# Converting 64-bit weights in blocks of 512 columns instead of 256, with two temporaries in the dead halves of the words

## The chip, the cores and the metric

The kernel runs on one core of a Trainium2 chip. The metric is the device time of one execution in microseconds (us), median over runs.

## What is computed

Attention with a feature map, then an ELU network whose weights come as float64, then a mixture of four experts (no biases):

```python
# attention: 4 batches, 8 heads, 576 tokens, 64 dims, 128 features
proj = einsum('bhsd,df->bhsf', x, w_phi);  proj -= max(abs(proj), -1)
phi = concatenate([exp(proj), exp(-proj)], -1)          # of q and of k
num = q_p @ (k_p^T v);  den = q_p @ sum(k_p) + 1e-6;  x = num / den
# ELU network: 2304 tokens, 512 -> 2048 -> 512, w_in and w_out float64
h = x @ w_in
g = where(h > 0, h, exp(minimum(h, 0)) - 1)
x = (g @ w_out).astype(float32)
# experts: E = 4, 512 -> 1024 -> 512, p = domain_probs normed
out += p[:, e:e+1] * (maximum(x @ w1[e], 0) @ w2[e])
```

## The kernel before

Activations and weights that TensorE multiplies are mostly split into a high part (fp32r) and the rest, so a product is three matmuls.

**Attention** works on 16 pairs of heads (`pair`, L171). A pair projects k and q (L194 in fp32 for the first seven pairs, L196 to L198 after), DVE takes the absolute maximum and subtracts it (`guard`, L204, L205, into `md`, `kp`, `qd`), ACT takes exponentials, TensorE forms k^T v (L237, L238), transposes q (L244) and forms numerator and denominator (L316), DVE divides (L325 reciprocal, L328 product into `xf`), and `put_x` splits `xf` into the tiles `xh` (ACT, L302) and `xl` (POOL, L303). A batch is four pairs.

**The ELU network** has 9 tiles of 256 tokens and runs in two halves of 4 units (`Elu`); a unit has 24 matmuls up (L525 to L527) and 24 down (L554 to L556). Between them ACT and DVE form `g` (L533, L534, L536) and its two parts `gh` (L537, ACT) and `gl` (L538, on POOL for the first three tiles, then on DVE). The down product of a unit is issued after the up product of the next. The first ELU unit needs the four pairs of batch 0.

**The experts** (`Up`, `Down`) fill the time from about 660 us on.

**Weights of the ELU network** are float64 in HBM, 32 tiles of 128 x 512 (16 of `w_in`, 16 of `w_out`). The chip has no float64 arithmetic here: `convert64` (L100) loads the words as 64-bit integers and builds the two fp32 parts from the upper and lower 32 bits, `hi` and `lo`, each of which is every other 32-bit word of the tile. Per block: one DMA (L102), ACT L108, L114 and L119, DVE L110 to L113, POOL L116, L118 and L121. `weight_stream` (L410) keeps up to `CVB` = 3 blocks in progress and advances one of them by a step at each call of `next(weights)`. Half of the 32 tiles fit in the ring of 16 (`RING`), so 32 blocks of 256 columns are converted at the start, beside attention, and the rest when the first half's weights are released, beside the last tiles of the first half and the start of the second. The calls come from two places: `PRE` calls at every step of attention until batch 0 is done (L747), then `WRATE` calls at every slot (L724).

The program is written as one stream; a scheduler of the tile framework then sets each engine's order of instructions, which all engines keep. Pools of buffers (`cv`, three of each tag) add waits: a load into `w64` waits for the last reader of the tile three blocks ago.

Of the kernel before, what the change touches and what calls it, by code (L numbers as in the profile page):

```python
# [8 lines left out]
F32 = mybir.dt.float32  # L9
F32R = mybir.dt.float32r  # L10
U32 = mybir.dt.uint32
I64 = mybir.dt.int64
ACTF = mybir.ActivationFunctionType
ALU = mybir.AluOpType
# [5 lines left out]
P = 128  # L20
# [24 lines left out]
LAG = 1  # L45
RING = 16
ATT_LAG = 5
PRE = 2
RATE = 1.4
WRATE = 2  # L50
CVB = 3
TAIL = 3
NF32 = 7
LDB = 1
CVP = 16
CVW = 256
CVOFF = 0
MINF = 2.0 ** -15
MAXF = 122879.9921875
# [3 lines left out]
def attn_elu_moe_kernel(ctx: ExitStack, tc: tile.TileContext, kq_in, vv, w_phi, w_in, w_out, probs, w1, w2, out):  # L63
    nc = tc.nc
    V, A, G, PE, SP = nc.vector, nc.scalar, nc.gpsimd, nc.tensor, nc.sync
    on = {'V': V, 'G': G}

    def f32(ap):
        return ap.bitcast(F32)

    def pool(name, bufs=1, stack=ctx, **kw):
        return stack.enter_context(tc.tile_pool(name=name, bufs=bufs, reuse_waits="tile", **kw))
# [14 lines left out]
    cv = pool("cv", CVB, stack=right, side="right")  # L87
# [12 lines left out]
    def convert64(dst, src, adder):  # L100
        st = cv.tile([P, CVW], I64, tag="w64", name="w64")
        SP.dma_start(st, src)  # L102
        words = st.bitcast(U32).rearrange("p (n two) -> p n two", two=2)
        lo, hi = words[:, :, 0], words[:, :, 1]
        top = cv.tile([P, CVW], U32, tag="top", name="top")
        pw = cv.tile([P, CVW], U32, tag="pw", name="pw")
        low = cv.tile([P, CVW], F32, tag="low", name="low")
        A.activation(f32(top), f32(hi), ACTF.Abs)  # L108
        yield
        V.tensor_scalar(out=f32(top), in0=f32(top), scalar1=MINF, scalar2=MAXF, op0=ALU.max, op1=ALU.min)  # L110
        V.tensor_scalar(out=top, in0=top, scalar1=3, scalar2=0x3FFFFFF8, op0=ALU.logical_shift_left, op1=ALU.bitwise_and)
        V.scalar_tensor_tensor(out=top, in0=hi, scalar=0xC0000000, in1=top, op0=ALU.bitwise_and, op1=ALU.bitwise_or)
        V.tensor_scalar(out=pw, in0=top, scalar1=0xFF800000, scalar2=None, op0=ALU.bitwise_and)  # L113
        A.activation(low, lo, ACTF.Copy, scale=2.0 ** -52)  # L114
        yield
        G.tensor_tensor(out=low, in0=low, in1=f32(pw), op=ALU.mult)  # L116
        yield
        adder.tensor_tensor(out=f32(top), in0=f32(top), in1=low, op=ALU.add)  # L118
        A.activation(dst[:, 0], f32(top), ACTF.Copy)  # L119
        yield  # L120
        G.tensor_tensor(out=dst[:, 1], in0=f32(top), in1=f32(dst[:, 0]), op=ALU.subtract)  # L121
# [241 lines left out]
    def ring_tile(key):  # L363
        rings[key] = ring.tile([P, 2, 512], F32R, tag="w", name="w")
        users.append(key)
# [34 lines left out]
    def conversions():  # L400
        for u in range(FP):
            for nm, src in (("in", w_in), ("out", w_out)):
                for f in (2 * u, 2 * u + 1):
                    while not room():
                        yield None
                    ring_tile((nm, f))
                    for o in range(0, 512, CVW):
                        yield convert64(rings[nm, f][:, :, o:o + CVW], src[f][:, o:o + CVW], G if f < CVP else V), (nm, f, o)

# [308 lines left out]
    def slot():  # L718
        quota[0] += rate[0]
        while quota[0] >= 1:  # L720
            quota[0] -= 1
            if done[0] < limit[0]:
                next(stream, None)
        for _ in range(WRATE):  # L724
            next(weights, None)
# [19 lines left out]
    while done[0] < NP:  # L745
        next(stream)
        for _ in range(PRE):  # L747
            next(weights)
# [134 lines left out]
```

## Time and profile before

| | us |
|---|---|
| median of three runs (1425.01 to 1426.37) | 1425.17 |
| the profiled execution | 1424.05 |
| its span, first to last instruction | 1422.3 |
| TensorE busy | 1380.5 |
| DVE busy | 698.2 |
| ACT busy | 619.9 |
| POOL busy | 446.7 |

The granted clock of TensorE is 0.997 of full speed over the span. PE is TensorE's matmuls and PEld its weight loads; DVE is VectorE, ACT ScalarE, POOL GpSimd, SP the engine that issues the DMAs. Matmuls are pipelined, so their spans overlap: a busy PE can still run below its pace. Spans on POOL are rough. A group's "idle before" says what the engine had been waiting for.

### The profile page before, as it was taken

What the parts mean: (1) busy time and instruction counts of PE and PEld (TensorE: products, weight loads), DVE (VectorE), ACT (ScalarE), POOL (GpSimd) and SP (SyncE); (2) the same over time, 40 slices, a digit from 0 to 9 for tenths busy, and PEclk for the clock granted to TensorE, in tenths of its full rate; (3) what the DMA queues carried; (4) which work ended last, traced back from release to release, by engine and by line L of the source; (5) the groups of instructions that cost most, each with busy time, mean ns of one, the idle gap of its engine ahead of it and who ended that gap; (6) DMA issues with size and microseconds to landing.
All of it is one profiled execution on the core that took longest, in us unless ns stands there. A gap on an engine that the chain in (4) does not pass through costs nothing.

```text
span 1422.3 us, 22325 instructions
## 1 busy us (share of the span) xinstructions
PE 1380.5 (97%) x8688; PEld 1286.9 (90%) x8688; DVE 698.2 (49%) x1150; ACT 619.9 (44%) x1348; POOL 446.7 (31%) x499
## 2 busy tenths in 40 slices
PE   7889999999999999999999999999999999999998
PEld 6788999999988999998898989898888989899897
DVE  7998856575588534333434323234432325323332
ACT  6777776665656544343333443122421214322121
POOL 5567654434588512033102350002320004300000
PEclk9999999999999999999999999999999999999999
DMA  5433222120423345313333233434145251433421
GB/s 162 128 118 117 88 66 77 40 74 24 128 90 118 112 143 191 108 46 104 114 131 148 94 106 135 160 112 148 45 149 181 105 196 52 141 111 133 167 78 67
DMA packets 93625, 160.22 MB, mean 113 GB/s; under 512 B 28496, under 2 KB 39888, under 8 KB 93520
## 3 DMA queue, kind: packets, MB, share of 16 engines
q1 hardware_dynamic: 93520, 158.80, 33.7%
q8 instruction: 68, 1.11, 0.3%
q14 instruction: 37, 0.30, 0.1%
HBM read 109.22 MB, written 49.55 MB: 112 GB/s over the span
## 4 chain that ended last, share of the span: by engine, by line
PE 74%; DVE 11%; DMA 5%; POOL 4%; issue 3%; ACT 3%; SPq 0%; DVEq 0%; POOLq 0%; ACTq 0%
PE bank L701 8%; PE bank L702 8%; PE bank L703 8%; PE bank L642 8%; PE bank L643 7%; PE bank L644 7%; PE bank L555 3%; PE bank L556 3%; PE bank L554 3%; PE bank L527 3%; PE bank L525 3%; PE bank L526 3%; PE bank L237 2%; PE bank L316 2%; DMA wst<-in_w 2%
## 5 line engine op out<-in xcount | busy, mean ns | idle before, releaser
L701 PE MATMUL bank<-w,h 128*128 128x512 f32 x576 | 224.5, 392 | 4.0 <-ACT h L653 4.0
L642 PE MATMUL bank<-xv,w 128*128 128x384 f32 x672 | 224.3, 340 | 3.1 <-ACT cm L648 2.9
L643 PE MATMUL bank<-xv,w 128*128 128x384 f32 x672 | 226.6, 337 | 0.0
L702 PE MATMUL bank<-w,h 128*128 128x512 f32 x576 | 225.5, 392 | 0.0
L644 PE MATMUL bank<-xv,w 128*128 128x384 f32 x672 | 223.4, 338 | 0.0
L703 PE MATMUL bank<-w,h 128*128 128x512 f32 x576 | 198.3, 391 | 0.7 <-DVE h L654 0.7
L462 POOL TENSOR_TENSOR w<-wst,w 128x256 fp32r<-128x256 f32 x80 | 62.2, 796 | 341.0 <-ACT w L461 336.9
L555 PE MATMUL bank<-gl,w 128*128 128x256 f32 x576 | 162.3, 286 | 6.3 <-DVE gl L538 5.0
L556 PE MATMUL bank<-gh,w 128*128 128x256 f32 x576 | 160.9, 284 | 0.0
L554 PE MATMUL bank<-gh,w 128*128 128x256 f32 x576 | 156.3, 288 | 3.9 <-ACT gh L537 3.4
L642 PEld LDWEIGHTS bank<-xv,w 128*128 128x128 f32 x672 | 126.6, 188 | 11.1 <-ACT cm L648 3.5
L654 DVE SCALAR_TENSOR_TENSOR h<-bank,h 128x384 fp32r<-128x384 f32 x144 | 77.4, 554 | 115.1 <-ACT h L653 115.1
L653 ACT ACTIVATE h<-bank 128x384 fp32r<-128x384 f32 x144 | 66.8, 490 | 151.6 <-PE bank L644 91.7
L701 PEld LDWEIGHTS bank<-w,h 128*128 128x128 f32 x576 | 108.5, 188 | 25.1 <-ACT h L653 5.3
L643 PEld LDWEIGHTS bank<-xv,w 128*128 128x128 f32 x672 | 126.8, 189 | 4.4
L702 PEld LDWEIGHTS bank<-w,h 128*128 128x128 f32 x576 | 108.6, 189 | 20.6
L644 PEld LDWEIGHTS bank<-xv,w 128*128 128x128 f32 x672 | 126.3, 188 | 0.0
L703 PEld LDWEIGHTS bank<-w,h 128*128 128x128 f32 x576 | 107.3, 188 | 20.0 <-DVE h L654 1.6
L555 PEld LDWEIGHTS bank<-gl,w 128*128 128x128 f32 x576 | 110.1, 191 | 9.6 <-DVE gl L538 7.5
L554 PEld LDWEIGHTS bank<-gh,w 128*128 128x128 f32 x576 | 106.1, 191 | 6.8 <-ACT gh L537 6.5
L556 PEld LDWEIGHTS bank<-gh,w 128*128 128x128 f32 x576 | 110.1, 191 | 0.2
L648 ACT ACTIVATE cmab<-bank 128x384 f32<-128x384 f32 x48 | 23.6, 492 | 178.0 <-PE bank L644 178.0
(119 smaller groups left out, 2991.0 us busy)
## 6 DMA issues: line engine op xcount, KB each, us to landing
xv<-xvd SPq DMA_DIRECT2D x42, 768.0 KB, 4.4
wst<-in_w SPq DMA_DIRECT2D x64, 256.0 KB, 2.8
xvd<-xv SPq DMA_DIRECT2D x21, 768.0 KB, 4.4
yscr<-y SPq DMA_DIRECT2D x54, 256.0 KB, 2.3
y<-yscr SPq DMA_DIRECT2D x54, 256.0 KB, 2.9
w<-in_w_in SPq DMA_DIRECT2D x32, 256.0 KB, 2.8
w<-in_w_out SPq DMA_DIRECT2D x32, 256.0 KB, 3.0
kq<-in_kq SPq DMA_DIRECT2D x16, 320.0 KB, 3.0
```

What stands on the lines that cost most here:

```text
L462: on[WL[v % len(WL)]].tensor_tensor(out=lo, in0=x, in1=f32(hi), op=ALU.subtract)
L554: PE.matmul(o, w[:, 0, c], self.gh[:, j], start=start, stop=False)
L555: PE.matmul(o, w[:, 0, c], self.gl[:, j], start=False, stop=False)
L556: PE.matmul(o, w[:, 1, c], self.gh[:, j], start=False, stop=stop)
L642: PE.matmul(o, hi[:, c], x[:, 0, kc], start=not more and kc == 0, stop=False, skip_group_check=more)
L643: PE.matmul(o, hi[:, c], x[:, 1, kc], start=False, stop=False, skip_group_check=more)
L644: PE.matmul(o, lo[:, c], x[:, 0, kc], start=False, stop=kc == 1, skip_group_check=more)
L653: A.activation(h[:, 0], c, ACTF.Relu)
L654: V.scalar_tensor_tensor(out=h[:, 1], in0=c, scalar=0.0, in1=f32(h[:, 0]), op0=ALU.max, op1=ALU.subtract)
L701: PE.matmul(self.acc, h[:, 0, c], w[:, 0], start=f == 0, stop=False)
L702: PE.matmul(self.acc, h[:, 0, c], w[:, 1], start=False, stop=False)
L703: PE.matmul(self.acc, h[:, 1, c], w[:, 0], start=False, stop=f == 2 * NQ - 1)
```

## The change

A block has 512 columns (`CVW`), a whole weight tile, so there are 32 blocks instead of 64 and each of the ten instructions handles twice the columns. The temporaries `pw` and `low` are gone: L113 writes the power of two into `hi`, which nobody reads after L112, and L114 writes the scaled low word over `lo`, in place; L116 and L118 read and write there. So the loaded tile is in use until L118, where it was free after L112 and L114. `PRE` and `WRATE` go from 2 to 1, which keeps the columns per call. `WRATE` also paces the later preparation of `w1` and `w2`. In the changed file all lines from 106 on have numbers lower by two.

```diff
-PRE = 2
+PRE = 1
-WRATE = 2
+WRATE = 1
-CVW = 256
+CVW = 512
...
         top = cv.tile([P, CVW], U32, tag="top", name="top")
-        pw = cv.tile([P, CVW], U32, tag="pw", name="pw")
-        low = cv.tile([P, CVW], F32, tag="low", name="low")
         A.activation(f32(top), f32(hi), ACTF.Abs)
         yield
...
         V.scalar_tensor_tensor(out=top, in0=hi, scalar=0xC0000000, in1=top, op0=ALU.bitwise_and, op1=ALU.bitwise_or)
-        V.tensor_scalar(out=pw, in0=top, scalar1=0xFF800000, scalar2=None, op0=ALU.bitwise_and)
-        A.activation(low, lo, ACTF.Copy, scale=2.0 ** -52)
+        V.tensor_scalar(out=hi, in0=top, scalar1=0xFF800000, scalar2=None, op0=ALU.bitwise_and)
+        A.activation(f32(lo), lo, ACTF.Copy, scale=2.0 ** -52)
         yield
-        G.tensor_tensor(out=low, in0=low, in1=f32(pw), op=ALU.mult)
+        G.tensor_tensor(out=f32(lo), in0=f32(lo), in1=f32(hi), op=ALU.mult)
         yield
-        adder.tensor_tensor(out=f32(top), in0=f32(top), in1=low, op=ALU.add)
+        adder.tensor_tensor(out=f32(top), in0=f32(top), in1=f32(lo), op=ALU.add)
```

The scheduler orders the instructions anew. TensorE has the same 8242 rows in both programs, in another order among the first 3134; the last 5108, from the first units of the second ELU half on, are the same. Three places:

**DVE, around the last divide of pair 0.** `top` and `pw` are tiles of `convert64`, `w_...` are loaded 64-bit tiles (from here on the changed file's L108 to L111 are L110 to L113), `rc`, `xf`, `qd` and `md` belong to attention. Before:

```order
L110 TENSOR_SCALAR top<-top 128x256
L205 TENSOR_TENSOR qd_298<-bank,mx 128x512
L328 TENSOR_TENSOR xf<-bank,rc 64x288 x2
L112 SCALAR_TENSOR_TENSOR top<-w_494,top 128x256
L204 TENSOR_REDUCE mx<-bank 128x2
L111 TENSOR_SCALAR top<-top 128x256
L113 TENSOR_SCALAR pw<-top 128x256
L205 TENSOR_TENSOR md<-bank,mx 128x256
L112 SCALAR_TENSOR_TENSOR top<-w_539,top 128x256
L204 TENSOR_REDUCE mx<-bank 128x4
L113 TENSOR_SCALAR pw<-top 128x256
```

and with the change:

```order
L108 TENSOR_SCALAR top<-top 128x512 x2
L326 TENSOR_TENSOR xf<-bank,rc 64x288 x2
L203 TENSOR_TENSOR qd_278<-bank,mx 128x512
L109 TENSOR_SCALAR top<-top 128x512 x2
L110 SCALAR_TENSOR_TENSOR top<-w_471,top 128x512
L110 SCALAR_TENSOR_TENSOR top<-w_531,top 128x512
L111 TENSOR_SCALAR w_471<-top 128x512
L108 TENSOR_SCALAR top<-top 128x512
L111 TENSOR_SCALAR w_531<-top 128x512
L109 TENSOR_SCALAR top<-top 128x512
L110 SCALAR_TENSOR_TENSOR top<-w_620,top 128x512
L111 TENSOR_SCALAR w_620<-top 128x512
```

Three whole blocks of 512 columns now stand together there, ahead of the next pair's `md`. Ahead of the 14th L328 (pair 3's first half) there are 65 rows of L110 to L113 in the order before and 52 of twice the width in the new one; 19 blocks of 512 columns are through DVE by the seventh pair, 35 of 256 before.

**DVE in the second conversion,** from one unit's L536 to the next. Before:

```order
L536 SCALAR_TENSOR_TENSOR g<-g,bank 128x512
L110 TENSOR_SCALAR top<-top 128x256
L111 TENSOR_SCALAR top<-top 128x256
L112 SCALAR_TENSOR_TENSOR top<-w_5360,top 128x256
L538 TENSOR_TENSOR gl<-g,gh 128x512
L113 TENSOR_SCALAR pw<-top 128x256
L110 TENSOR_SCALAR top<-top 128x256
L111 TENSOR_SCALAR top<-top 128x256
L112 SCALAR_TENSOR_TENSOR top<-w_5422,top 128x256
L113 TENSOR_SCALAR pw<-top 128x256
L110 TENSOR_SCALAR top<-top 128x256
L111 TENSOR_SCALAR top<-top 128x256
```

and with the change (L534 and L536 are L536 and L538 before):

```order
L534 SCALAR_TENSOR_TENSOR g<-g,bank 128x512
L108 TENSOR_SCALAR top<-top 128x512
L109 TENSOR_SCALAR top<-top 128x512
L536 TENSOR_TENSOR gl<-g,gh 128x512
L110 SCALAR_TENSOR_TENSOR top<-w_5121,top 128x512
L111 TENSOR_SCALAR w_5121<-top 128x512
L108 TENSOR_SCALAR top<-top 128x512
L109 TENSOR_SCALAR top<-top 128x512
L110 SCALAR_TENSOR_TENSOR top<-w_5219,top 128x512
```

Two conversion rows instead of three stand ahead of `gl`. In the bulk of this stretch ten rows of 256 columns stood between two units; now 52 rows of 512 columns stand in ten units.

**SP, at the load of `kq` for pair 2** (L136 and L139 before, L134 and L137 after; L102 loads a block, the rows into `vt` are v). Before:

```order
L102 DMA w_433<-in_w_out 128x256
L142 DMA vt_168<-in_vv 128x4x64
L144 DMA vt_168<-in_vv 64x64
L102 DMA w_494<-in_w_out 128x256
L102 DMA w_539<-in_w_in 128x256
L136 DMA kq<-in_kq 128x640
L139 DMA kq<-in_kq 128x512
```

and with the change:

```order
L102 DMA w_376<-in_w_out 128x512
L140 DMA vt_168<-in_vv 128x4x64
L142 DMA vt_168<-in_vv 64x64
L102 DMA w_471<-in_w_in 128x512
L102 DMA w_531<-in_w_in 128x512
L134 DMA kq<-in_kq 128x640
L137 DMA kq<-in_kq 128x512
```

The `kq` load stands behind blocks of twice the size, each of which waits for a tile that is now in use until L118.

## Rows read from the trace of the kernel before

**Rows 1.** Page, busy us, share of the span and instructions of each engine.

```profile
PE 1380.5 (97%) x8688; PEld 1286.9 (90%) x8688; DVE 698.2 (49%) x1150; ACT 619.9 (44%) x1348; POOL 446.7 (31%) x499
```

**Rows 2.** Busy us and count by stretch: PE, PEld, DVE, ACT, POOL, clock, DMA share, GB/s.

```profile
0.00:79.00 79.00, 63.40 (x376) 54.98 (x377) 71.11 (x138) 56.02 (x140) 45.12 (x67) 1.00 0.48 145
79.00:178.00 99.00, 94.55 (x707) 89.21 (x707) 83.30 (x153) 70.74 (x169) 69.68 (x86) 1.00 0.34 104
...
356.00:391.60 35.60, 35.60 (x301) 35.60 (x300) 20.99 (x38) 22.11 (x45) 19.02 (x20) 1.00 0.42 128
391.60:427.20 35.60, 32.45 (x249) 30.12 (x248) 31.98 (x61) 20.51 (x49) 29.14 (x36) 1.00 0.29 93
427.20:462.80 35.60, 32.22 (x251) 30.34 (x250) 31.45 (x58) 24.66 (x57) 28.73 (x37) 1.00 0.35 115
```

**Rows 3.** Waits of PE, 0 to 79 us: total us, times, longest us.

```profile
PE bank L244 <- DVE qd L205: 10.3, 6, 3.4
```

**Rows 4.** Waits of PE, 375 to 468 us.

```profile
PE bank L555 <- DVE gl L538: 3.5, 7, 1.0
```

**Rows 5.** Groups of DVE, 0 to 79 us: count, busy us, mean ns, idle before.

```profile
L112 DVE SCALAR_TENSOR_TENSOR top<-w,top 128x256 uint32<-128x256 uint32 x16 | 9.0, 565 | 0.2
L110 DVE TENSOR_SCALAR top<-top 128x256 f32<-128x256 f32 x17 | 7.5, 441 | 1.0 <-ACT top L108 0.9
L205 DVE TENSOR_TENSOR kp<-bank,mx 128x512 f32<-128x512 f32 x10 | 6.7, 680 | 0.0
...
L111 DVE TENSOR_SCALAR top<-top 128x256 uint32<-128x256 uint32 x16 | 5.4, 345 | 0.1
...
L113 DVE TENSOR_SCALAR pw<-top 128x256 uint32<-128x256 uint32 x16 | 4.9, 312 | 0.1
...
L205 DVE TENSOR_TENSOR md<-bank,mx 128x256 f32<-128x256 f32 x5 | 2.1, 418 | 0.0
```

**Rows 6.** Groups of DVE, 79 to 178 us.

```profile
L112 DVE SCALAR_TENSOR_TENSOR top<-w,top 128x256 uint32<-128x256 uint32 x19 | 11.2, 606 | 0.2
...
L111 DVE TENSOR_SCALAR top<-top 128x256 uint32<-128x256 uint32 x19 | 8.9, 484 | 0.2
L113 DVE TENSOR_SCALAR pw<-top 128x256 uint32<-128x256 uint32 x19 | 8.4, 459 | 0.1
L110 DVE TENSOR_SCALAR top<-top 128x256 f32<-128x256 f32 x18 | 6.0, 352 | 3.2 <-ACT top L108 2.9
```

**Rows 7.** Groups of DVE and, below the dots, POOL, 375 to 468 us.

```profile
L112 DVE SCALAR_TENSOR_TENSOR top<-w,top 128x256 uint32<-128x256 uint32 x29 | 19.4, 670 | 0.5
L111 DVE TENSOR_SCALAR top<-top 128x256 uint32<-128x256 uint32 x29 | 15.8, 546 | 0.7
...
L110 DVE TENSOR_SCALAR top<-top 128x256 f32<-128x256 f32 x29 | 12.8, 445 | 8.3 <-ACT top L108 8.3
L113 DVE TENSOR_SCALAR pw<-top 128x256 uint32<-128x256 uint32 x29 | 12.5, 434 | 0.6
...
L118 POOL TENSOR_TENSOR top<-top,low 128x256 f32<-128x256 f32 x29 | 24.0, 830 | 0.8
```

**Rows 8.** Timeline, DVE and POOL: start us, us, engine, line, operation.

```profile
142.71 1.35 POOL L184 TENSOR_TENSOR sl<-kq,sh 128x512 fp32r<-128x512 f32 x1
...
142.94 1.27 DVE L111 TENSOR_SCALAR top<-top 128x256 uint32<-128x256 uint32 x1
...
417.43 0.29 DVE L113 TENSOR_SCALAR pw<-top 128x256 uint32<-128x256 uint32 x1
...
417.80 0.73 POOL L116 TENSOR_TENSOR low<-low,pw 128x256 f32<-128x256 f32 x1 [0.69 <-DVE pw L113]
...
417.96 0.72 DVE L111 TENSOR_SCALAR top<-top 128x256 uint32<-128x256 uint32 x1
```

**Rows 9.** Timeline, PE, the first matmul of an ELU unit.

```profile
79.20 0.36 PE L525 MATMUL bank<-xh,w 128*128 128x256 f32 x1
```

**Rows 10.** Waits of the DMA queue SP, 0 to 178 us.

```profile
SPq L102 <- DVE top L112: 67.3, 31, 7.3
```

## The prediction, made before the changed kernel ran

> **What bounds the kernel now.** Start with the busy line of the page: TensorE is busy 97% of a span of 1422.3 us, and no other engine is over half [rows 1]. A change to the conversion of weights can only win back time in which TensorE waits, so the next view is the table of stretches [rows 2]. In the stretch 356 to 391.6 us TensorE is busy throughout; it is not in 0 to 79, 79 to 178, 391.6 to 427.2 and 427.2 to 462.8 us, and those are the stretches in which `convert64` runs. In three of the four DVE is busy about nine tenths of the time, in 79 to 178 us 83.3 of 99.
>
> How much is really lost there? Matmuls of one product overlap, so a busy TensorE can still be slowed. Count instead: 35.6 us without conversions hold 301 matmuls, 0.118 us each; the two slices with them hold 249 and 251 [rows 2]. 102 matmuls are missing, 12.1 us, where the busy column shows 6.5 us of idle time (3.15 and 3.38), 1.86 times as much. By the same ratio the 4.45 us of idle in 79 to 178 us (99 less 94.55) stand for about 8.3 us (an estimate, the mix of matmuls is another there).
>
> Who is late? Up to 79 us the transposes of L244 wait 10.3 us for `qd`, which DVE writes at L205 [rows 3]. In the second conversion L555 waits for `gl`, DVE's L538 [rows 4]. So both stretches hang on **DVE's queue**, in which conversions stand ahead of what TensorE needs. POOL is next: 29.1 of 35.6 us in the second one [rows 2].
>
> **Cost of one conversion on DVE.** Per 256 columns the four operations L110 to L113 take 441 + 345 + 565 + 312 = 1663 ns up to 79 us [rows 5], 352 + 484 + 606 + 459 = 1901 ns from 79 to 178 us [rows 6], and 445 + 546 + 670 + 434 = 2095 ns in the second conversion [rows 7]. So 512 columns cost 3.33, 3.80 and 4.19 us now. What joining two of them saves is read from L205: 128x256 takes 418 ns, 128x512 takes 680 ns [rows 5], so one instruction of 512 columns is 156 ns cheaper than two of 256. Four operations save 0.62 us, and 512 columns cost 2.70, 3.18 and 3.57 us. That is the value I take; it leaves the waits as they are per column.
>
> Its ends come from those waits. L113 takes 0.29 us when POOL is idle; L111 takes 0.72 us when it starts inside a POOL operation of 0.73 us, and 1.27 us inside one of 1.35 us, which has 512 columns: it ends just after POOL's does [rows 8]. After the change all three POOL operations of a block have 512 columns. If no operation waited, three would take about 0.42 us (0.29 and half of the 0.26 that 256 more columns add at L205) and L112 about 0.68 us like L205: 1.94 us per 512. If three of four waited through a POOL operation of 1.35 us and one didn't, it is 3 x 1.27 + 0.42 = 4.2 us. I take the middle, since today's means of L110, L111 and L113 (434 to 546 ns [rows 7]) lie between 0.29 and 0.72 us too.
>
> The Trainium skill, "Advanced Engine Details and Errata", section "VectorE Performance Modes", notes that GPSIMD instructions and Vector instructions that use two ports block each other. The trace agrees [rows 8]; by that rule, which speaks against longer POOL operations, one gets the upper end, the second and third rival below.
>
> L113 now writes every other word instead of a dense tile; no row has a DVE operation that does. If it ran at L205's pace it took 0.68 instead of 0.42 us, 0.26 us more per block; I take 0.42 and keep this for the range. "VectorE: DVE Perf Modes" of the Trainium skill, section "What auto-detection actually checks", asks for one source, both sides in SBUF and even outer dimensions, not for dense words; by it L113 keeps its rate, which no run here shows yet.
>
> **Up to the first ELU matmul** (79.20 us [rows 9]). It needs pair 3's first `xf`, the 13th and 14th L328. By the order, 65 conversion rows stand ahead of that on DVE before, and 52 after: 13 blocks of 512 columns instead of 16 of 256, so 10 blocks' worth (of 256) more columns are done early; the first excerpt shows where. Now that is 9.0 + 7.5 + 5.4 + 4.9 = 26.8 us [rows 5]; then 13 x 2.70 = 35.1 us. DVE is full (71.1 of 79 us, and most of the rest is the start), so the first ELU matmul comes **8.3 us later**, with ends of -1.5 (13 x 1.94) and +16.5 us (13 x 3.33, no saving).
>
> **From there to 178 us.** Now 11.2 + 8.9 + 8.4 + 6.0 = 34.5 us of conversions [rows 6]; then 6 blocks, 6 x 3.18 = 19.1 us, so DVE has 15.4 us less to do. TensorE cannot win more than the 8.3 us it loses here; I take 7. The first stretch nets **+1.3 us**.
>
> **The second conversion.** Now 19.4 + 15.8 + 12.8 + 12.5 = 60.5 us for 29 blocks [rows 7]; then 13 x 3.57 = 46.4 us. By the order (second excerpt) some ten conversion rows stand between two of L536 now, 10 x 0.52 = 5.2 us, and 52 rows over ten units afterwards, 5.2 x 0.89 = 4.6 us. A unit (48 matmuls) loses 12.1 us / 10.4 units = 1.16 us now; 0.6 us of it goes, ten times: **-6 us**, with ends 0 and -12.1 us.
>
> **ACT, POOL, DMA.** ACT's three and POOL's three operations per block get fewer in the same way: POOL's now take 0.83 us each in the second conversion [rows 7], so 5.0 us per 512 columns, and at the 1.35 us of [rows 8] it is 4.05 us. Neither engine sets the pace of TensorE by the waits shown, so I cost them at nothing; if POOL ran slower on alternate words, its cover ends where one operation costs 1.66 us, twice the present. L116 and L118 touch alternate words, and no row has that on POOL. The halves of the 64-bit tile are now held until L118 has read `lo`. The loads of L102 wait for that tile; today for DVE's L112, 67.3 us in 31 waits [rows 10]. That is harmless as long as nothing is queued behind them on SP, but the `kq` loads are (third excerpt), and that is a rival. From the second half of the ELU stage on, TensorE's rows are the same 5108 in both, so the halved `WRATE` moves nothing there and costs nothing.
>
> **Sum.** 8.3 - 7 - 6 = -4.7 us. The profiled execution took 1424.05 us, 1.75 us more than its span, and lies 1.1 us under the median of the runs, 1425.17. So 1419.3 us against it, and 1420.5 us against the median.
>
> **The rivals.** About 0.2%, 2.85 us, is what a measurement of this kernel can tell from no change.
>
> *Slower: the early conversions are not paid back.* The columns that DVE does before the first ELU matmul grow by 60% and each operation waits out a longer POOL operation. Place: DVE up to 79 us. Price: 13 x 3.33 = 43.3 us, 16.5 us late, 7 back by 178 us, half of the second gain (-3): +6.5, 1431.7 us. It decides where a conversion row averages over 0.75 us in that stretch. For it: DVE is full there, and 1.27 us in [rows 8]. Against: POOL is busy only 45 of 79 us [rows 2]. Chance 0.20.
>
> *No change: POOL sets DVE's pace in the second conversion.* Three of four DVE operations wait, 4.2 us per 512 columns as worked out above, against 4.19 now: no gain, and 1.3 us of loss from the first stretch, 1426.5 us. For it: POOL is busy 82% there. Against: its operations leave gaps today. Chance 0.25.
>
> *Slower: `kq` comes late.* L102 now waits for L118, at least two POOL operations (2.7 us) after L113. Three `kq` loads stand right behind such an L102 before the first ELU matmul: up to 8 us, with nothing won back of it: 1428.5 us. Against: there is one block of 512 where two of 256 waited. Chance 0.05.
>
> *Much faster.* The waits vanish with the instructions, DVE is at 1.94 us per 512 columns, the first ELU matmul is not later, and 7 + 6 us return, half as much again in the second: some -13, 1412 us. Chance 0.08, since POOL does not go away.
>
> **How the numbers follow.** The forecast has 0.42. Faster takes it and the last rival: 0.50. Within 0.2%: 0.25. Slower: 0.20 + 0.05. The likeliest single case is the forecast, 1420.5 us. Its own range, 1414 to 1423, comes from 0 to -12 in the second stretch and L113's rate in the first. For 8 in 10 the range reaches to the two larger rivals and part of the smallest: 1411 to 1432 us.
>
> **What would show it.** Right: the first L525 (L523 in the changed file) starts between 84 and 91 us instead of 79.2; the slices that answer to 391.6 to 462.8 us hold over 270 matmuls each; the group of L110 (L108 then) averages 0.5 to 0.7 us. Wrong: the first L525 at or before 79 us (the early conversions cost nothing), or conversion rows over 0.9 us in the first 80 us (POOL's length rules), or `kq` among the releasers of TensorE or ACT in the first 100 us. Wrong too if time moves after 500 us, where I expect none.

## The result, and the profile after

The changed kernel takes **1433.04 us** (median of four runs, 1432.63 to 1434.62), the kernel before 1425.09 us beside it: a ratio of 1.0057, 95% interval 1.0039 to 1.0074. It is slower by 8 us, where 1420.5 us was forecast, and lies 1 us above the upper end of the range. The profiled execution took 1432.91 us and has a span of 1431.1 us.

First the page's busy line and the stretches of time of the changed kernel (columns as in [rows 2], of which these are the counterparts):

```profile
PE 1384.2 (97%) x8688; PEld 1295.9 (91%) x8688; DVE 687.0 (48%) x1022; ACT 608.7 (43%) x1252; POOL 425.1 (30%) x403
...
0.00:79.00 79.00, 57.41 (x296) 50.83 (x297) 67.73 (x105) 51.13 (x104) 46.00 (x47) 0.87 0.49 153
79.00:178.00 99.00, 94.27 (x677) 88.62 (x677) 75.19 (x109) 64.95 (x141) 56.94 (x52) 0.98 0.35 108
...
391.60:427.20 35.60, 33.69 (x281) 33.32 (x280) 32.61 (x40) 19.72 (x35) 26.81 (x20) 1.00 0.24 79
427.20:462.80 35.60, 30.37 (x236) 29.71 (x235) 32.49 (x35) 21.58 (x39) 27.09 (x21) 0.95 0.31 104
```

DVE has 128 instructions less and is busy 687.0 us instead of 698.2 [rows 1], so the work did shrink. But up to 79 us TensorE is busy 57.41 us where it was 63.40, with 296 matmuls instead of 376, and its granted clock is 0.87 instead of 1.00 [rows 2]. Of the two slices of the second conversion one holds 281 matmuls (249 before), the other 236 (251 before); the changed kernel is 13 us behind by then, so the slices do not hold quite the same work.

TensorE's waits up to the first ELU matmul, and that matmul in the timeline:

```profile
PE bank L242 <- DVE qd L203: 17.9, 5, 5.8
...
96.78 0.37 PE L523 MATMUL bank<-xh,w 128*128 128x256 f32 x1
```

It starts at 96.78 us; [rows 9] has 79.20, so it is **17.6 us later** than before, and the transposes wait 17.9 us for `qd` on the way (10.3 us up to 79 us in [rows 3]).

How much of that is given back? The start of an ELU unit's first matmul can be set against the same unit before. Unit 1 is 17.6 us late, unit 4 15.2, unit 12 (229 us) and unit 29 (395 us) 13.2, unit 49 (520 us) 9.1, unit 69 9.5, and the last matmul of all 8.9. So 4.4 us come back while attention runs on, nothing between 229 and 395 us, 4.1 us in the second conversion, nothing after it. 17.6 - 4.4 - 4.1 = 9.1.

The conversion's groups on DVE (13 blocks, all that stand ahead of the 14th divide), against [rows 5], and below the dots POOL's three:

```profile
L110 DVE SCALAR_TENSOR_TENSOR top<-w,top 128x512 uint32<-128x512 uint32 x13 | 11.6, 899 | 0.1
L109 DVE TENSOR_SCALAR top<-top 128x512 uint32<-128x512 uint32 x13 | 10.6, 819 | 0.0
L111 DVE TENSOR_SCALAR w<-top 128x512 uint32<-128x512 uint32 x13 | 9.0, 694 | 0.1
...
L108 DVE TENSOR_SCALAR top<-top 128x512 f32<-128x512 f32 x13 | 6.7, 522 | 3.8 <-ACT top L106 3.8
...
L116 POOL TENSOR_TENSOR top<-top,w 128x512 f32<-128x512 f32 x12 | 16.3, 1362 | 0.2
L119 POOL TENSOR_TENSOR w<-top,w 128x512 fp32r<-128x512 f32 x11 | 14.5, 1322 | 8.1 <-ACT w L117 8.1
L114 POOL TENSOR_TENSOR w<-w 128x512 f32<-128x512 f32 x12 | 13.7, 1142 | 19.0 <-DVE prs L95 9.8 <-DVE w L111 8.7 <-issue 0.4
```

One block costs DVE 899 + 819 + 694 + 522 = 2934 ns; 2.70 us was taken. These means mix two kinds of rows, as DVE and POOL in the timeline show:

```profile
60.26 0.42 DVE L111 TENSOR_SCALAR w<-top 128x512 uint32<-128x512 uint32 x1
...
61.88 1.29 POOL L116 TENSOR_TENSOR top<-top,w 128x512 f32<-128x512 f32 x1
61.89 1.56 DVE L109 TENSOR_SCALAR top<-top 128x512 uint32<-128x512 uint32 x1
...
67.20 1.03 POOL L114 TENSOR_TENSOR w<-w 128x512 f32<-128x512 f32 x1
67.23 1.30 DVE L111 TENSOR_SCALAR w<-top 128x512 uint32<-128x512 uint32 x1
```

None of the 29 conversion rows that start outside a POOL operation, up to the 14th divide, takes over 0.43 us (0.70 us for L110); all 20 rows that take over a quarter more than the median of these start inside one, and the two above end 0.28 and 0.30 us after POOL's does. So the 38.2 us that the 13 blocks take are 25.1 us of rows at the length that they have outside, and **13.1 us of waits** beyond it. Counted the same way, the 27.1 us before are 20.5 us and 6.6 us. And the same in the second conversion, against [rows 7]:

```profile
L110 DVE SCALAR_TENSOR_TENSOR top<-w,top 128x512 uint32<-128x512 uint32 x13 | 18.5, 1421 | 0.2
...
L111 DVE TENSOR_SCALAR w<-top 128x512 uint32<-128x512 uint32 x13 | 11.0, 847 | 0.3
L109 DVE TENSOR_SCALAR top<-top 128x512 uint32<-128x512 uint32 x13 | 11.0, 846 | 0.4
L108 DVE TENSOR_SCALAR top<-top 128x512 f32<-128x512 f32 x13 | 10.3, 790 | 2.5 <-ACT top L106 2.5
...
L119 POOL TENSOR_TENSOR w<-top,w 128x512 fp32r<-128x512 f32 x16 | 23.4, 1468 | 5.3 <-ACT w L117 5.2
L116 POOL TENSOR_TENSOR top<-top,w 128x512 f32<-128x512 f32 x13 | 20.6, 1584 | 0.2
L114 POOL TENSOR_TENSOR w<-w 128x512 f32<-128x512 f32 x13 | 14.9, 1145 | 13.6 <-DVE w L111 13.6
```

1421 + 847 + 846 + 790 = 3904 ns per 512 columns; 4.19 us before, 3.57 us forecast. Here 25.3 of the 50.8 us are such waits; before it was 24.4 of 60.8 us.

### The profile page after: what moved, and what is told of

Read it like the earlier page. It is cut to its first block, busy times and chain, and to the rows that moved or that the text cites. A ratio compares the mean times of both kernels' runs of the same rounds, so it can differ in the third digit from the quotient of the medians.

```text
span 1431.1 us, 21937 instructions
## 1 busy us (share of the span) xinstructions
PE 1384.2 (97%) x8688; PEld 1295.9 (91%) x8688; DVE 687.0 (48%) x1022; ACT 608.7 (43%) x1252; POOL 425.1 (30%) x403
## 4 chain that ended last, share of the span: by engine, by line
PE 83%; DVE 8%; DMA 4%; issue 3%; ACT 1%; POOL 1%; SPq 0%; DVEq 0%; POOLq 0%; ACTq 0%
PE bank L699 9%; PE bank L700 9%; PE bank L701 8%; PE bank L640 8%; PE bank L641 8%; PE bank L642 8%; PE bank L553 4%; PE bank L554 4%; PE bank L552 4%; PE bank L525 4%; PE bank L523 4%; PE bank L524 4%; PE bank L235 4%; PE bank L314 3%; DVE top L110 2%
## 5 line engine op out<-in xcount | busy, mean ns | idle before, releaser
L554 PE MATMUL bank<-gh,w 128*128 128x256 f32 x576 | 161.4, 284 | 0.0
L640 PEld LDWEIGHTS bank<-xv,w 128*128 128x128 f32 x672 | 126.5, 188 | 10.9 <-ACT cm L646 3.7
L699 PEld LDWEIGHTS bank<-w,h 128*128 128x128 f32 x576 | 108.5, 188 | 24.6 <-ACT h L651 4.8
L700 PEld LDWEIGHTS bank<-w,h 128*128 128x128 f32 x576 | 108.6, 189 | 20.5
L554 PEld LDWEIGHTS bank<-gh,w 128*128 128x128 f32 x576 | 111.0, 193 | 0.1
```

Source lines behind the costliest of these rows:

```text
L554: PE.matmul(o, w[:, 1, c], self.gh[:, j], start=False, stop=stop)
L640: PE.matmul(o, hi[:, c], x[:, 0, kc], start=not more and kc == 0, stop=False, skip_group_check=more)
L699: PE.matmul(self.acc, h[:, 0, c], w[:, 0], start=f == 0, stop=False)
L700: PE.matmul(self.acc, h[:, 0, c], w[:, 1], start=False, stop=False)
```

## The experiments

Three theories were set against each other. **A:** what sets the start of the first ELU matmul is how much DVE has to convert ahead of it in its order, and that comes from the columns in progress (`CVB` blocks times `CVW` columns), not from their width as such. **B:** it is the length of the operations: a DVE operation of 512 columns waits out a POOL operation of 512. **C:** it is the loaded tile, now held until POOL's sum, so that loads and what is queued with them come late.

`CVB` is also the number of buffers that each tile of `convert64` has, so blocks in progress and buffers change together in every run that sets it; only the extra `w64` tile of e9 and e11 parts the two. The columns ahead are counted in halves of 256 columns that stand on DVE ahead of the 14th divide (L328 before, L326 after), in each kernel's order. Since `PRE` and `WRATE` always went with the width (columns per call), they have no column. "Conversion" and "idle" are DVE's time in the four conversion lines, and with nothing running, up to the start of that divide, in the profiled execution. The units' delays are against the kernel before. A ratio is against the kernel before in the same set of runs (1423.85 to 1425.09 us).

| kernel | width, in progress | ahead | first ELU matmul, us | conversion, idle, us | unit 29, unit 49 late, us | time, us | ratio, 95% interval |
|---|---|---|---|---|---|---|---|
| before | 256, 3 | 16 | 79.2 | 27.1, 7.9 | | 1425.09 | |
| changed | 512, 3 | 26 | 96.8 | 38.2, 11.7 | 13.2, 9.1 | 1433.04 | 1.0057 (1.0039 to 1.0074) |
| e2_inplace256 | 256, 3 | 16 | 78.5 | 25.6, 12.0 | 3.8, -0.3 | 1422.59 | 0.9988 (0.9977 to 0.9998) |
| e7_six256 | 256, 6 | 28 | 103.1 | 52.6, 8.4 | 17.9, 15.0 | 1437.76 | 1.0097 (1.0082 to 1.0112) |
| e3_two512 | 512, 2 | 20 | 90.1 | 26.0, 16.2 | 5.3, -1.0 | 1420.48 | 0.9973 (0.9963 to 0.9982) |
| e1_two512_separate | 512, 2 | 18 | 82.5 | 24.5, 12.0 | 4.3, -1.2 | 1422.07 | 0.9990 (0.9981 to 1.0000) |
| e9_two512_spare | 512, 2 | 20 | 92.2 | 27.4, 17.2 | 6.9, 0.4 | 1421.44 | 0.9981 (0.9970 to 0.9991) |
| e10_two512_low | 512, 2, low | 18 | 78.7 | 24.3, 10.7 | 0.0, -6.8 | 1416.57 | 0.9945 (0.9928 to 0.9962) |
| e11_two512_spare_low | 512, 2, low | 16 | 74.6 | 17.7, 10.2 | -1.4, -8.2 | **1415.08** | 0.9936 (0.9920 to 0.9951) |
| e8_two256 | 256, 2 | 11 | 73.7 | 15.7, 13.0 | 18.4, 29.2 | 1454.00 | 1.0211 (1.0193 to 1.0228) |
| e12_three512_low | 512, 3, low | 24 | 88.4 | 32.3, 8.9 | 4.3, 1.7 | 1425.39 | 1.0004 (0.9995 to 1.0014) |
| e13_before_low | 256, 3, low | 15 | 76.3 | 24.3, 10.1 | 8.4, 8.6 | 1434.46 | 1.0067 (1.0052 to 1.0082) |

**Half of the change: in place, but 256 columns** (e2_inplace256, from the changed kernel).

```diff
-PRE = 1
+PRE = 2
-WRATE = 1
+WRATE = 2
-CVW = 512
+CVW = 256
```

> The in-place temporaries alone: blocks of 256 columns, PRE and WRATE at 2, three blocks in progress. Theory A (columns ahead): DVE works off more columns before the first ELU matmul because three blocks of 512 are in progress instead of three of 256; this kernel has 16 blocks of 256 ahead of the 14th divide product on DVE as before, so first ELU matmul at 78 to 81 us and 1424 to 1427 us. Theory B (long operations): each DVE operation waits out a POOL operation of 512 columns; nothing is longer here, so also 1424 to 1427 us. Theory C (held tile): the loads now wait for POOL's sum (L116) instead of DVE's L110; then ACT and DVE starve here too: first ELU matmul at 84 us or later and 1429 us or more.

The first ELU matmul is back at 78.5 us and the time is 0.12% under before's, somewhat less than A and B had expected. Writing into the dead halves, with the tile held longer, costs nothing in the end, and C's numbers are missed. It is not free on the way: DVE is idle 4.1 us more, and unit 29 is 3.8 us late, which the second conversion gives back. So what hurts comes with the width, or with the columns that the width brings into progress.

**The same columns in progress as the changed kernel, but of 256** (e7_six256): the edit above and

```diff
-CVB = 3
+CVB = 6
```

> In place, blocks of 256 columns, but six of them in progress, as many columns as the change has in three; by the order 28 blocks of 256 stand ahead of the 14th divide product on DVE (16 before, 26 with the change). Theory A (columns ahead): first ELU matmul at 95 us or later, 28 blocks x 1.66 us being 20 us more than now, and 1432 us or more. Theory B (long operations): the early columns are paid back, only the width hurts: 1424 to 1428 us. Theory C (held tile): six tiles hide the wait for the sum, 1424 to 1428 us.

All operations are short again, and yet the first ELU matmul comes at 103.1 us and the kernel is slower than the changed one. Its waits of PE up to 178 us:

```profile
PE bank L242 <- DVE qd L203: 24.6, 5, 10.2
```

24.6 us for `qd` with 28 halves ahead, as A expected. The harm does not need long operations, so B is not needed for it; that long operations add a part in the changed kernel is not excluded.

**Wide, with fewer columns in progress** (e3_two512, from the changed kernel).

```diff
-CVB = 3
+CVB = 2
```

> The change with two blocks of 512 columns in progress instead of three; by the order 20 blocks' worth of 256 columns stand ahead of the 14th divide product (16 before, 26 with the change). Theory A: in proportion to the columns, first ELU matmul at 79 + 17.6 x 4/10 = 86 us and 1427 to 1430 us. Theory B: as slow as the change, 1432 to 1435 us. Theory C: with two tiles each load waits longer, worse than the change, 1434 us or more.

Faster than before by 0.27%, with the same wide instructions in place. All three theories missed the time: B and C had it as slow as the change, and A, which scaled the delay with the columns, had 86 us for the first ELU matmul and 1427 us or more. The first ELU matmul is 10.9 us late, although DVE spends no more time on conversions than before (26.0 against 27.1 us): here DVE is idle for 16.2 us. What ACT waits for up to 92 us, and a piece of the chain of waits (start us, us, what):

```profile
ACT w L117 <- POOL top L116: 8.8, 4, 2.3
ACT top L106 <- DMA w<-in_w_out: 5.4, 2, 4.1
...
ACT top L106 <- DMA w<-in_w_in: 2.7, 1, 2.7
...
51.54 0.88 PE bank L192 x4
...
52.43 0.33 SPq L134
...
53.29 0.02 SPq L102
...
53.40 5.29 DMA w<-in_w_out
...
58.77 0.66 ACT top L106
...
59.98 0.31 ACT xh L300
```

The weight load L102 is issued on SP behind a `kq` load (L134) that had waited for TensorE's L192, takes 5.3 us, and ACT's L106 stands waiting for it. Behind L106 and L112 in ACT's queue is attention's `xh` (L300), which starts at 59.98 us, though DVE had finished its `xf` at 57.5 us. So a conversion row that waits for its load, or for POOL, holds up attention's rows behind it, on ACT and from there on DVE. For the start, then, the columns ahead are one part, **where the waiting rows stand** is another.

**Separate temporaries, two blocks of 512** (e1_two512_separate, from the kernel before; three blocks of 512 with separate temporaries were not run).

```diff
-PRE = 2
+PRE = 1
-WRATE = 2
-CVB = 3
+WRATE = 1
+CVB = 2
-CVW = 256
+CVW = 512
```

> Blocks of 512 columns, two in progress, with the two temporaries in tiles of their own as before, so that a loaded tile is free after L112 and L114; 18 blocks' worth of columns ahead of the 14th divide product. Against the kernel with two blocks in place: theory A expects 1 to 2 us less (18 against 20 blocks ahead), 1426 to 1429 us; theory B the same time as that one, as the operations are as long; theory C at least 4 us less, and 1425 us or less.

1422.07 us with 18 halves ahead and the first ELU matmul at 82.5 us, 7.6 us ahead of e3's: two halves fewer, and 4.2 us less of idle DVE. Yet the end is 1.6 us later than e3's, so in place is not what costs. The expectations missed here too: A had this kernel 1 to 2 us ahead of e3, C at least 4 us. Whether the idle time of e3 comes from the tile being held is what the next kernel asks.

**A spare tile for the loads** (e9_two512_spare: e3 and a third `w64` buffer).

```diff
-        st = cv.tile([P, CVW], I64, tag="w64", name="w64")
+        st = cv.tile([P, CVW], I64, tag="w64", name="w64", bufs=3)
```

> The change with two blocks in progress (as the kernel that took 1420.5 us, first ELU matmul at 90.1 us) and a third buffer for the loaded 64-bit tile alone, so that a load no longer waits for POOL's sum of the block before last; 20 blocks' worth of 256 columns stand ahead of the 14th divide product on DVE, as there. Theory C (held tile): the late first ELU matmul there, 90.1 us against 82.5 us of the kernel with separate temporaries, is the loads' wait, so 83 to 86 us here and 1416 to 1419 us. Theory A (columns ahead): it is the columns (20 against 18), so 88 to 91 us and 1419 to 1422 us.

Nothing is gained: first ELU matmul at 92.2 us (A had 88 to 91), idle DVE 17.2 us, 1421.44 us. The spare tile did change what it was meant to: ACT waits 3.2 us in all for weight loads up to 92 us, where it waited 8.6 us in e3. DVE is idle as long all the same, so the late loads, C, are not the cause of e3's idle time.

**The conversions' rows later in the order** (e10_two512_low: e3; e11_two512_spare_low: e9, each with

```diff
-CVOFF = 0
+CVOFF = -300
```

which lowers the priority that the scheduler gives the rows of `convert64`).

> Two blocks of 512 in place at the lower priority, no spare tile: 18 blocks' worth ahead. Theory A: first ELU matmul at 82 to 86 us, 1416 to 1420 us. Theory C: the loads' wait stays, 87 us or later and 1420 us or more.

> As the kernel with the spare tile, with the conversions at a lower priority in the scheduler (CVOFF at -300): 16 blocks' worth of 256 columns ahead of the 14th divide product, exactly as in the kernel before the change, but as 8 blocks of 512. Theory A (columns ahead): the first ELU matmul is back at 77 to 81 us and the time at 1413 to 1419 us. Theory B (long operations): DVE operations wait out POOL operations of 512 columns, so 84 us or later and 1421 us or more.

Both beat both kernels: 1416.57 us and **1415.08 us, 0.64% under before**; the times are as A expected, the first ELU matmul comes 3.3 and 2.4 us ahead of its ranges. With 16 halves ahead, as many as before, e11 has the first ELU matmul at 74.6 us, and wide operations turn out cheaper. Its conversion groups on DVE up to 90 us, and below the dots its waits of PE up to 178 us:

```profile
L110 DVE SCALAR_TENSOR_TENSOR top<-w,top 128x512 uint32<-128x512 uint32 x10 | 7.1, 726 | 0.0
...
L111 DVE TENSOR_SCALAR w<-top 128x512 uint32<-128x512 uint32 x10 | 5.8, 593 | 0.0
L109 DVE TENSOR_SCALAR top<-top 128x512 uint32<-128x512 uint32 x10 | 4.6, 472 | 0.0
L108 DVE TENSOR_SCALAR top<-top 128x512 f32<-128x512 f32 x10 | 4.4, 437 | 0.1
...
PE bank L242 <- DVE qd L203: 5.8, 4, 1.7
PE bank L523 <- ACT w L117: 4.7, 1, 4.7
```

726 + 593 + 472 + 437 = 2228 ns per block against 2934 in the changed kernel and 3326 for the same columns before. Up to the 14th divide only 9 of its 32 conversion rows start inside a POOL operation (23 of 52 in the changed kernel), and 2.3 of their 17.7 us are waits. `qd` is waited for 5.8 us instead of 17.9. ACT's waits for weight loads are 3.2 us, no less than in e9, so they are not what the lower priority took away. What it took away is DVE's waits for ACT's L106: 4.4 us in e9, none here. The price appears at the other end: the weights of an early unit come late, 4.7 us at L523.

**Too few in progress** (e8_two256: the edit of e2 and `CVB = 2`).

> In place, two blocks of 256 columns in progress: 11 blocks ahead of the 14th divide product, fewer than before (16). Theory A in the other direction: first ELU matmul at 70 to 75 us, but the weights of the second to fourth unit come later, so TensorE waits between 80 and 178 us instead; 1422 to 1430 us. Theory B and C have nothing that would make it slower than the kernel before up to the first ELU matmul, and none that makes it faster there by more than 2 us.

The first ELU matmul is the earliest of all, 73.7 us, and the kernel the slowest, 1454.0 us. Its waits of PE from 90 to 178 us, and two stretches:

```profile
PE bank L552 <- ACT w L117: 9.8, 5, 7.6
...
98.00:108.00 10.00, 4.89 (x17) 4.24 (x18) 5.26 (x14) 3.79 (x10) 5.91 (x9) 0.50 0.30 99
...
121.00:139.00 18.00, 12.31 (x36) 9.45 (x37) 11.55 (x25) 6.98 (x19) 12.46 (x16) 0.53 0.22 81
```

With 11 halves done, the early units run out of weights (unit 4 is 18.8 us late). In the second conversion another 10.8 us are lost, there mostly in waits for `gh` (ACT's L535, 7.9 us from 375 to 515 us) and less for weights (3.7 us). A had the start right, 70 to 75 us, and the time far too low, 1430 us at most; B and C had nothing that would bring the start forward by more than 2 us, and it came 5.5 us earlier. So A alone is not "the fewer ahead, the better": there is a floor.

**Which part does priority play?** (e12_three512_low: the changed kernel with `CVOFF = -300`; e13_before_low: the kernel before with it.)

> The changed kernel with the conversions' scheduling priority lowered by 300 and nothing else: three blocks of 512 in place. By the order 24 half-blocks stand ahead of the 14th divide (26 without, 16 before). Theory A (what DVE has to convert ahead of the first ELU matmul sets its start): about 2 columns' blocks fewer, so the first ELU matmul at 88 to 95 us, the time at 1423 to 1430 us. Rival, priority alone (conversion rows that wait for a load no longer stand ahead of attention's rows, the number of columns ahead matters little): first ELU matmul near 79 us or before, and 1415 to 1419 us, like the two-block kernels with lower priority.

> The kernel before with the conversions' priority lowered by 300 and nothing else: 256 columns, separate temporaries, three blocks, 15 half-blocks ahead of the 14th divide instead of 16. If the gain of the two-block kernels with lower priority comes from priority alone, this gives 1415 to 1418 us too, and the first ELU matmul comes by 75 us. If wider operations are needed for it (3.6 us of DVE per 512 columns here against 2.5 there, and 4.2 against 3.2 in the second conversion), first ELU matmul at 75 to 78 us and 1420 to 1424 us, with the second conversion winning at most 2 us on the ELU units.

e12 gives what A expected, 88.4 us and 1425.39 us, the same as before within the interval; priority alone does not bring the changed kernel near e11. Of the 8.4 us that the first ELU matmul moves forward, one block less on DVE is 2.9 us, a lower price per block (32.3 us for 12, 2.69 each instead of 2.93) 2.9 us, and less idle time 2.8 us: 8.6 us, about the whole. e13 missed both expectations: its first ELU matmul comes at 76.3 us as the second one had it, but the kernel is slower than before by 0.67%. Its waits of PE up to 178 us (lines as in the kernel before), and the stretch of the longest:

```profile
PE bank L554 <- ACT gh L537: 6.2, 1, 6.2
...
110.20:116.70 6.50, 0.28 (x4) 0.08 (x2) 5.09 (x15) 5.46 (x14) 3.91 (x6) 0.70 0.23 77
```

TensorE does nearly nothing for 6.5 us ahead of a down product (L554), while conversion rows on ACT and DVE stand ahead of the `g` that this product waits for (between 111.7 and 115.3 us DVE runs ten of them, then `g`, L536); unit 3 is 3.6 us early, unit 4 is 8.2 us late, and the second conversion wins nothing back. Conversions cost e13 about what they cost before (3.7 us of DVE per 512 columns up to 178 us; 3.6 before, 2.5 in e11), and pushing them back has moved them into the ELU units. Lower priority paid with two wide blocks in progress (e10, e11) and with three (e12), and not with narrow ones (e13); that the lower price of the wide rows decides this is argued, not shown.

## Why the prediction was wrong

*What bounds the kernel.* Right: TensorE waits for DVE's queue in the same stretches, and the loss is made there. After 520 us the delay stays between 8.9 and 9.6 us, so the halved `WRATE` moves nothing, as predicted.

*The order.* Right in count: 13 blocks of 512 ahead of the 14th divide instead of 16 of 256, and the forecast costed the larger number. The runs show that this is the change's main effect, and that it comes from keeping `CVB` at 3 while each block doubles: e7 has it with narrow operations, e3 loses most of it with wide ones.

*The step that failed: "the first ELU matmul comes 8.3 us later".* It was 17.6. Its working was 13 x 2.70 - 26.8, and it made three assumptions that did not hold.

The first is the price: "it leaves the waits as they are per column". 13 blocks took 38.2 us, 2.93 us each and not 2.70, so the conversions alone add 11.1 us to the 27.1 that they took before. Joining two instructions did save what was forecast: rows outside POOL's operations take 1.28 us per 256 columns and 1.94 us per 512, 0.62 us less than two of 256. But the waits went from 0.81 to 1.01 us per 512 columns. About as many rows start inside a POOL operation (26 of 65 before, 23 of 52 now); what they wait there more than doubled, from 0.25 to 0.57 us a row.

The second, "DVE is full", and with it ACT costed "at nothing", is the larger fault: it lets DVE's own time be the whole delay. The other 6.5 us are not conversions. DVE was idle 3.8 us more, 2.9 of them waiting for ACT's L106, and it was busy 0.9 us longer than the added rows explain, since its records overlap less.

The third is that the first ELU matmul waits for the 14th divide. In e2 it starts 3.7 us ahead of that divide's start, and in the kernel before 0.7 us ahead of its end: the first nine matmuls of the unit read pairs 0 to 2, and only the tenth reads pair 3 (82.9 us before, 100.8 now). On TensorE it stands 20 matmuls behind the transposes of a `qd`, which DVE writes shortly ahead of the divide. Before, and below the dots now:

```profile
76.58 0.63 PE L244 MATMUL bank<-ident,qd 128*128 128x128 f32 x4 [1.99 <-DVE qd L205]
77.05 1.06 PE L237 MATMUL bank<-vt,kp 128*128 128x128 f32 x8
...
92.53 0.76 PE L242 MATMUL bank<-ident,qd 128*128 128x128 f32 x4 [2.94 <-DVE qd L203]
93.09 1.92 PE L235 MATMUL bank<-vt,kp 128*128 128x128 f32 x8
```

These transposes start 16.0 us later, by what DVE did, and the same rows then take 4.25 us up to the ELU matmul instead of 2.62: TensorE's granted clock was 1.2 GHz up to 96.3 us (below). That makes up the 17.6 us to within 0.2.

Where a row waits in its queue, the chain of waits of the changed kernel has it like this:

```profile
42.47 1.70 POOL top L116
44.18 3.32 DMA w<-in_w_out
47.52 0.69 ACT w L112
...
48.72 0.52 ACT kp L206
...
74.25 1.71 PE bank L235 x8
...
79.37 0.89 PE bank L235 x8
```

POOL's sum releases the tile, the load takes 3.3 us, ACT's L112 waits for it, and only behind it comes attention's `kp` (L206), whose input DVE had finished at 46.6 us. And TensorE, which had waited, ran eight L235 in 1.71 us at 74.25 us and in 0.89 us at 79.37 us: it was at the lower clock the first time (below). e12 is the test of the queue part: the same kernel, rows further back, 2.8 us less idle.

*"I take 7" of it back by 178 us.* 4.4 us came back (17.6 to 13.2), the last of it by 229 us. That DVE has less to do later is right (75.19 us busy instead of 83.30 from 79 to 178 us), but a unit that starts late wins only where TensorE was waiting.

*"-6 us" in the second conversion.* It was -4.1. The price per 512 columns fell to 3.90 us, not 3.57: joining saved 0.55 us, and the waits grew from 1.68 to 1.95 us, most of all in L110 (1421 ns). But e2 also wins 4.1 us between units 29 and 49, with 256 columns and 4.31 us of DVE per 512. So the saving by joined instructions, by which the step was worked out, is not shown to be what won them; each kernel has its own order there, and which part is the order stays open. Two blocks of 512 in place do better: DVE 3.2 us and POOL 4.0 us per 512 columns, waits of 1.2 to 1.3 us, and 6.3 (e3) to 6.8 us (e10, e11) won. With two in separate tiles (e1) it is 3.8 us, waits of 1.9 us, and 5.5 us won, so the number in progress alone does not set the price.

*The rivals.* "Slower: the early conversions are not paid back" was the one that came, 1431.7 us worked out and 1433.04 measured; it had 16.5 us late, 7 and 3 back, against 17.6, 4.4 and 4.1. That it came so near is partly luck. Its 16.5 us were to be DVE's rows alone, which added 11.1 us (0.73 us a row, under its condition of 0.75); the rest came from the queue's waits, which it left out too. Its mechanism, that each operation waits out a longer POOL operation, holds for the rows that start inside one. Its chance of 0.20 was too low: the time that a waiting row adds on its queue had no term at all. "POOL sets DVE's pace": no, its condition was no gain at 4.2 us per 512 columns; 3.90 us were measured and 4.1 us won. "`kq` comes late": L102 does wait for POOL now, 17.4 us in 8 waits up to 97 us,

```profile
SPq L102 <- POOL top L116: 17.4, 8, 4.0
```

but no `kq` load is among what releases TensorE or ACT in that stretch.

*Its signs.* Of those for "right" only L108's mean came, 522 ns; the first ELU matmul was not between 84 and 91 us, and one slice of the second conversion held 236 matmuls, not over 270. One of those for "wrong" came: of the 55 conversion rows in the first 80 us 12 take over 0.9 us. Two slips: the lower end of the first step is -1.6, not -1.5, and "the second and third rival" that go by blocking are the first and the second.

*L113's alternate words.* L111 (L113 before) takes 413 ns at the least and 422 at the median of 13: 0.42 us, the value taken, and L109, which writes a dense tile, takes as long outside POOL's operations: no loss of rate for writing every other word. The Trainium skill, "VectorE: DVE Perf Modes", section "What auto-detection actually checks", does not ask for dense words; the trace agrees.

## What to carry to other kernels

When a block of background work grows, scale the number of blocks in progress down with it: in these runs the product of both set, for the most part, how much of it the scheduler placed ahead of the urgent work. Then put its rows later in the order, since on an in-order queue a row that waits for a load or another engine stops all behind it; stop where the consumer of the background work begins to wait. To price such a change, count rows ahead of the first urgent instruction on each engine, and price a row in two parts: what it takes with the other engines silent, which joining makes cheaper, and what it waits, which joining can make dearer.

## What the runs showed of the hardware

TensorE's granted clock fell from 2.4 GHz to half, the 1.2 GHz level, five times in the first 100 us of the changed kernel, and once more at 427 us; before, it did so nowhere ahead of 660 us. Two such stretches (the clock is the third number from the end of a row):

```profile
31.40:38.20 6.80, 3.43 (x16) 3.46 (x17) 6.72 (x12) 3.38 (x9) 5.07 (x6) 0.50 0.45 152
...
72.40:79.20 6.80, 6.04 (x27) 5.89 (x28) 6.69 (x11) 4.36 (x9) 3.42 (x3) 0.50 0.49 181
```

Around each of these TensorE had been waiting for `qd`: 5.8 us up to 34.8 us, 3.3 us up to 73.2 us. The kernel before has waits of 3.4 us (up to 13.7 us) and 2.0 us (up to 51.2 us) and stays at 2.4 GHz there, so the length of one wait does not tell it. Three groups of eight L235 in the chain up to 97 us take 1.71 us and a fourth, in which the clock rises, 1.37 us, against 0.89 us at 2.4 GHz: 2.9 us, an estimate from these rows. In the last stretch, ahead of the first ELU matmul, it is 1.6 us of the delay, by the same 24 matmuls in both kernels (4.25 and 2.62 us). What the clock costs in all was not tried by itself.

POOL on alternate words is not slow: L114, with its operands and its result on every other word, takes 1142 ns for 512 columns, less than L119 with 1322 ns, which writes dense words (spans on POOL are rough).

A conversion row on DVE is slow only where it starts inside a POOL operation. In all twelve traces, up to the 14th divide, none of the rows of L108, L109 and L111 that start outside one takes over 0.43 us at 512 columns or 0.30 us at 256 (L110: 0.70 and 0.43 us). So one block costs DVE 2.2 us in e11 and 2.9 us in the changed kernel by the same instructions: 0.3 us of a block's time are waits there, 1.0 us here.
